# Clustered attention and token mixing: transposes of the row maxima two units later, logits two units earlier, a weight chunk converted in six stages instead of four

## The chip, the cores and the metric

The kernel runs on one core of one Trainium2 chip. The metric is the device time in microseconds (us) of one execution; of several, the median is given. Five engines run their own instruction queues in order and wait for one another through semaphores: PE (TensorE, matrix products), DVE (VectorE), ACT (ScalarE), POOL (GpSimd), and SP (SyncE), which here issues nearly all DMAs.

## The reference

```python
def _attn_ref(q, k, v, centroids):          # q, k, v: 4 x 8 heads x 768 x 64, float32
    q_n = q / (norm(q) + 1e-06); k_n = ...; c_n = ...      # 16 centroids for each head
    q_assign = argmax(einsum('bhsd,hcd->bhsc', q_n, c_n), -1)
    k_assign = argmax(einsum('bhsd,hcd->bhsc', k_n, c_n), -1)
    mask = q_assign[:, :, :, None] == k_assign[:, :, None, :]
    scores = where(mask, scale * q @ k.T, -1e9)
    attn = exp(scores - max(scores, -1))
    return (attn / (sum(attn, -1) + 1e-09)) @ v

def _moe_ref(x, w_theta, w_tok_r, w_tok_i, w_ch):   # x: the heads side by side, 4 x 768 x 512
    theta = x @ w_theta
    y = einsum('ts,bsd->btd', w_tok_r, x * cos(theta)) + einsum('ts,bsd->btd', w_tok_i, x * sin(theta))
    u = x + y
    return u + maximum(u @ w_ch, 0.0)
```

A query sees only the keys that fall to the same centroid. The four weight matrices arrive as float64.

## The kernel before

**Pairs and units.** The 32 heads are worked off as 16 pairs of heads, one head on partitions 0 to 63 and the other on 64 to 127. A pair has 12 *units*: two halves of 384 queries, each against six tiles of 128 keys. For a unit PE makes the scores of 128 keys by 384 queries for both heads (`sc`, four products: high and low parts of q and k, and a product of `mk` and `mq` that carries the mask and the row maximum), ACT takes the exponential into `at`, POOL adds up `at` tiles into `acc` for the softmax sums, and PE multiplies `at` with v (`av`). All of PE's work on one pair lasts some 30 us.

**The maxima, 12 units ahead.** The row maximum is subtracted inside the scores product, so it is made one pair ahead (`LEAD = 12`): PE makes `m` (128 queries by 768 keys), DVE reduces it (`nm`, L364). After three turns of the loop the six columns of a half are complete; `shift_row` (L368) transposes them on PE (`mt`, L372), ACT copies them (`mr`, L374) and two small DMAs write them as a row into `mq` (L376). The first scores product of that half reads the row.

**The loop.** One turn of the loop at L561 takes two units. PE's order in a turn is: the scores of the first unit for both heads; the second unit's scores of head 0 beside an `m` of head 1; eight `av` products; the extra work that is due at the even unit; the second unit's scores of head 1 beside an `m` of head 0; the extra work due at the odd unit. In what follows a turn is named by its even unit within the pair: turn 0, 2, 4, 6, 8, 10. The functions `at_unit` and `stages` put the extra work into a table by unit; a generator's stages are run up to the next `yield`, one for each number of a tuple. `in_order` (L507) then pins the program order on every engine, so that order, and nothing else, is what each queue runs.

**The extra work of a pair**, by unit within the pair (P is the pair whose scores run): 

- assignment to centroids (`assign`, `A_UNITS`), for P+3: load of q and k (`raw`) at 4, logits `lg` (L248) and their copy `lgs` at 8, transposes `lt` (L259) with `mxl` and `eq` (L262, L264) at 10, `eq` times weights and `rr` (L268, L270) at 11; for P+2: `rt` (L292) and `ri` at 2, DMA `rd` at 3, four DMAs `clq`/`clk` at 4, `mq` (L305) at 7, `mk` (L307) at 9;
- high and low parts of q and k of P+2: ACT copies at 0 and 2 (L324), POOL subtractions `lq` at 2 and `lk` at 4 (L328);
- `shift_row` at 6 (first half of P+1) and at 0 (second half of P); the load of v at 7;
- softmax sums of P-1: `sm` on PE and `se` on ACT at 4, small DMAs at 6, 8, 9 and 10; the scaling of the result of P-2 on POOL (L472) at 1 and its DMA at 3;
- one weight chunk (`early_weights`, 14 chunks, `to_f32` and `split_w`): DMA of the float64 words at 0; at 4 the magnitude on ACT (`Abs`, L132), a clamp (L133) and a shift (L135) on DVE; at 6 two bit operations on DVE (L138, L140); at 8 the rounded high part on ACT (L149) and the low part on POOL (L150). Eight chunks have 512 columns (`w_theta`, `w_ch`), six have 768.

**Buffers that matter here.** The tiles `m`, `lg`, `lt`, `rt`, `mt` and `sm` take turns in one pool of two PSUM buffers (`m_tile`, through `bank`): a tile can be written once the tile before the last has been read. The scores have three PSUM banks. `raw` has three buffers, so the load of a pair's k waits for the POOL subtraction `lq` of the pair before. A chunk's float64 words and its result have one buffer each.

After the 16 pairs the mixing stage follows (L596 on): for each 128-token tile theta, sine and cosine, two mixing products (`y`) and the channel product (`cp`, `cy`).

Of the kernel before, what the change touches and what calls it, by code (L numbers as in the profile page):

```python
# [21 lines left out]
LEAD = 12  # L22
# [18 lines left out]
def kernel(  # L41
# [23 lines left out]
    NT = S // P  # L65
# [49 lines left out]
    def to_f32(src, cols, new):  # L115

        raw, w = new()
        w = w[:, 0:cols]
        if src.dtype == F32:
            nc.sync.dma_start(out=w, in_=src)
            return w
        raw = raw.bitcast(I32)[:, 0:2 * cols]
        nc.sync.dma_start(out=raw, in_=src.bitcast(I32))
        raw = raw.rearrange("p (n t) -> p n t", t=2)
        low, high = raw[:, :, 0], raw[:, :, 1]
        wi = w.bitcast(I32)  # L130
        yield
        nc.scalar.activation(out=w, in_=high.bitcast(F32), func=AF.Abs)  # L132
        nc.vector.tensor_scalar(  # L133
            out=w, in0=w, scalar1=F64_LEAST, scalar2=F64_MOST, op0=ALU.max, op1=ALU.min)
        nc.vector.tensor_scalar(  # L135
            out=wi, in0=wi, scalar1=5, scalar2=2, op0=ALU.logical_shift_left, op1=ALU.logical_shift_right)
        yield
        nc.vector.scalar_tensor_tensor(  # L138
            out=wi, in0=low, scalar=29, in1=wi, op0=ALU.logical_shift_right, op1=ALU.bitwise_or)
        nc.vector.scalar_tensor_tensor(  # L140
            out=wi, in0=high, scalar=-(1 << 30), in1=wi, op0=ALU.bitwise_and, op1=ALU.bitwise_or)
        return w

    def split_w(hi, lo, src, cols, new, eng, most):

        def chunk(sl):
            w = yield from to_f32(src[:, sl], sl.stop - sl.start, new)
            yield
            nc.scalar.copy(out=hi[:, sl], in_=w)  # L149
            eng.tensor_tensor(out=lo[:, sl], in0=w, in1=hi[:, sl].bitcast(F32), op=ALU.subtract)  # L150

        n = cols // -(-cols // most)
        return [chunk(slice(c0, c0 + n)) for c0 in range(0, cols, n)]
# [21 lines left out]
    for x in range(3):  # L175
        x = (NPAIR + x) % 3
# [242 lines left out]
    def sums(pi):  # L419

        s = st[pi]
        sm = bank(f"sm{pi}")[:, 0:HS]
        for x in range(NT // TERMS):
            for j in range(2):
                for a in range(2):
                    g = 2 * j + a
                    nc.tensor.matmul(  # L427
                        sm[32 * g:32 * g + 32], lhsT=ecol, rhs=s["acc", a, x][:, j],
                        start=(x == 0), stop=(x == NT // TERMS - 1))
        se = p2.tile([P, HS], F32, tag="se", name=f"se{pi}", bufs=1)  # L430

        if pi < NPAIR - 1:
            nc.scalar.activation(out=se, in_=sm, func=AF.Identity, bias=eps)
        else:
            last_sum[0] = nc.vector.tensor_scalar_add(se, sm, 1e-9)
        yield

        sd = [dram.tile([4, HS], F32, tag=f"sd{x}", name=f"sd{x}{pi}", bufs=2) for x in range(2)]
        over = [x.rearrange("g (r n) -> (g r) n", r=32) for x in sd]
        nc.sync.dma_start(out=sd[0], in_=se.rearrange("(g r) n -> g r n", r=32)[:, 0])  # L440
        yield
        sq = p2.tile([P, 4 * HS // P], F32, tag="sq", name=f"sq{pi}")
        nc.sync.dma_start(out=sq, in_=over[0])
        yield
        nc.vector.reciprocal(out=sq, in_=sq)
        nc.sync.dma_start(out=over[1], in_=sq)
        yield
        s["rb"] = p1.tile([P, 2, HS], F32, tag="rb", name=f"rb{pi}")
        for j in range(2):
            last_load[0] = nc.sync.dma_start(  # L450
                out=s["rb"][64 * j:64 * j + 64],
                in_=sd[1][2 * j:2 * j + 2].unsqueeze(0).broadcast_to([64, 2, HS]))
# [15 lines left out]
    def normalise(pi):  # L468
        b, p = divmod(pi, NP)
        s = st.pop(pi)  # L470

        (nc.gpsimd if pi < NPAIR - 2 else nc.vector).tensor_tensor(  # L472
            out=s["xt"], in0=s["xt"], in1=s["rb"], op=ALU.mult)
        yield
        nc.sync.dma_start(out=xT_d[b][:, p], in_=s["xt"].rearrange("p a s -> p (a s)"))

    def early_weights():
        for c in range(NCT):
            yield from split_w(*w_th[c], w_theta[c * P:(c + 1) * P], DM, raw_pair, nc.gpsimd, CKE)
        for t in range(EARLY):  # L480
            for w, src in ((w_r, wrT), (w_i, wiT)):
                yield from split_w(*w[t], src[t * P:(t + 1) * P], S, raw_pair, nc.gpsimd, CKE)
        for c in range(NCT):
            yield from split_w(*w_c[c], w_ch[c * P:(c + 1) * P], DM, raw_pair, nc.gpsimd, CKE)
# [8 lines left out]
    def at_unit(u, fn, *a):  # L493
        todo.setdefault(u, []).append((fn, a))

    def stages(units, gen):

        for u in units:
            at_unit(u, lambda: next(gen, None))
        at_unit(units[-1] + 1, run, gen)  # L500
# [15 lines left out]
                tail[ins.engine] = ins.name  # L516


    A_UNITS = (-8, -4, -2, -1, 2, 3, 4, 7, 9)
    HI_UNITS = dict(q=0, k=2)  # L520
    LO_UNITS = dict(q=2, k=4)
    W_UNITS = (4, 6, 8)
    W_EVERY = 12
    def prepare(pi, gen):
        u = NU * (pi - 2)
        stages([u + k + (4 if pi == 1 and k < 0 else 0) for k in A_UNITS[1 if pi == 1 else 0:]], gen)
        for n in "qk":
            at_unit(u + HI_UNITS[n], part_hi, pi, n)
            at_unit(u + LO_UNITS[n], part_lo, pi, n, nc.gpsimd)
# [14 lines left out]
    for pi in range(NPAIR):  # L544
        u = NU * pi
        if pi > 0:
            prepare(pi, g1 if pi == 1 else assign(pi))
            at_unit(u - NU + 7, load_v, pi)
        for a in range(2):
            at_unit(u + a * NT - LEAD + NT, shift_row, pi, a)  # L550
        stages([u + NU + k for k in SUMS], sums(pi))
        stages([u + NU + k for k in NORM], normalise(pi))
    for x, gen in enumerate(early_weights()):
        u = W_EVERY * x
        stages([u] + [u + k for k in W_UNITS], gen)


    idle = ps_av.tile([P, 512], F32, tag="av", name="idle")
# [1 line left out]
    u = -LEAD  # L560
# [175 lines left out]
    def add_y(b, c0, c1):  # L736

        xT, n = xts[b], c1 - c0
        uh, ul = (u_tile(f"u{x}{b}_{c0}")[:, :, 0:n] for x in "hl")
        for d in range(NCT):  # L740
            x = xT[:, d, c0:c1]
            for n0, n1, _ in cuts(b, d, c0, c1):
                nc.vector.tensor_tensor(
                    out=xT[:, d, n0:n1], in0=y_at(b, d, n0, n1), in1=xT[:, d, n0:n1], op=ALU.add)
            nc.scalar.copy(out=uh[:, d, :], in_=x)  # L745
            nc.gpsimd.tensor_tensor(out=ul[:, d, :], in0=x, in1=uh[:, d, :].bitcast(F32), op=ALU.subtract)  # L746
        return uh, ul
# [54 lines left out]
    u = None  # L802
    for part in range(S // PW):
# [4 lines left out]
        u = add_y(B - 1, part * PW, (part + 1) * PW)  # L808
# [28 lines left out]
def _build(arrays):  # L837
    import concourse.bacc as _bacc
    import concourse.tile as _tile
    from concourse import mybir as _mybir  # L840

    nc = _bacc.Bacc("TRN2", target_bir_lowering=False, num_devices=1)
    args = []
    for name in _NAMES:
        a = arrays[name]
        args.append(nc.dram_tensor(f"in_{name}_dram", a.shape, _mybir.dt.from_np(a.dtype), kind="ExternalInput").ap())
    B, H, D, S = arrays["qT"].shape
    args.append(nc.dram_tensor("out_0_dram", (B, H * D, S), _mybir.dt.float32, kind="ExternalOutput").ap())
    with _tile.TileContext(nc, schedule_with_timeline_sim=True) as tc:
        kernel(tc, *args)  # L850
    return nc
# [10 lines left out]
```

## Time and profile before

| | |
|---|---|
| median of 3 runs | 877.84 us (877.35 to 878.13) |
| the profiled execution | 880.9 us, its span 879.1 us |
| mean granted TensorE clock | 0.979 |
| lead-in of the maxima | from about 14 to 37 us of the span |
| units of the 16 pairs | from about 37 to 497 us |
| mixing stage at a steady pace | from about 572 us to the end |

The page gives busy time by engine, then the span in 40 slices of 22 us, then the chain of work that ended last. In the views by instruction each row has the start in the span, the duration, the engine, the line, output and inputs, and in brackets the idle time of the engine before it with what ended it. `PEld` is the weight load of a matrix product.

### The profile page before, as it was taken

How to read it: one execution, taken by the hardware profiler on the slowest of the kernel's cores; microseconds unless marked ns; L12 is line 12 of the kernel's file. 1: busy time of each engine (PE TensorE's matmuls, PEld its weight loads, DVE VectorE, ACT ScalarE, POOL GpSimd, SP SyncE). 2: the span in 40 equal slices, each digit the busy share in tenths (PEclk: the TensorE clock that was granted, in tenths of full speed). 3: DMA queues.
4: the chain of work that ended last, by engine and by line, in shares of the span. 5: the costliest groups of instructions: out<-in, count | busy, mean ns of one | idle time of the engine just before them, and what ended most of it. 6: DMA issues, size and time to landing. Idle time of an engine off the chain costs nothing.

```text
span 879.1 us, 14379 instructions
## 1 busy us (share of the span) xinstructions
PE 813.5 (93%) x5688; PEld 594.2 (68%) x5688; DVE 501.3 (57%) x660; ACT 383.2 (44%) x787; POOL 462.7 (53%) x298
## 2 busy tenths in 40 slices
PE   4899989898898899889899989999999999999998
PEld 2465555555555555555555547789888988899998
DVE  5686676678668667766864158944333442253322
ACT  3255554555554455455544456453233323323220
POOL 3186767677785786767576646454122412241231
PEclk9699999999999999999999998999999999999999
DMA  2122322322331332232223135200300030001001
GB/s 92 55 80 89 107 61 85 117 93 82 118 113 50 113 118 63 98 99 85 74 68 118 47 122 167 73 1 1 144 1 1 11 133 1 1 27 46 1 7 67
DMA packets 29648, 62.21 MB, mean 71 GB/s; under 512 B 8932, under 2 KB 14156, under 8 KB 29196
## 3 DMA queue, kind: packets, MB, share of 16 engines
q1 hardware_dynamic: 29436, 60.89, 21.3%
q8 instruction: 45, 0.74, 0.3%
q10 hardware_dynamic: 144, 0.39, 0.1%
q14 instruction: 23, 0.19, 0.1%
HBM read 48.20 MB, written 12.96 MB: 70 GB/s over the span
## 4 chain that ended last, share of the span: by engine, by line
PE 71%; DVE 19%; issue 4%; ACT 3%; DMA 2%; POOL 0%; SPq 0%; DVEq 0%; POOLq 0%; ACTq 0%
PE y L732 20%; PE sc L342 12%; PE av L460 11%; PE m L342 7%; PE tp L665 6%; DVE nm L364 6%; PE cy L755 4%; DVE w L133 3%; PE sm L427 3%; DVE eq L268 2%; PE cp L755 2%; PE lg L248 2%; ACT w L132 1%; DVE eq L264 1%; DVE mxl L262 1%
## 5 line engine op out<-in xcount | busy, mean ns | idle before, releaser
L364 DVE TENSOR_REDUCE nm<-m 128x1 f32<-128x768 f32 x192 | 181.2, 952 | 93.6 <-PE m L342 82.6
L395 ACT ACTIVATE at<-sc 128x384 f32<-128x384 f32 x384 | 172.1, 491 | 111.3 <-PE sc L342 78.1
L406 POOL TENSOR_TENSOR acc<-at,at 128x768 f32<-128x768 f32 x64 | 120.3, 1880 | 122.4 <-ACT at L395 122.4
L342 PE MATMUL m<-hk,hq 64*128 64x384 f32 x384 | 150.0, 404 | 12.0 <-DVE nm L364 11.9
L460 PE MATMUL av<-at,vt 128*64 128x384 f32 x768 | 146.3, 501 | 0.0
L406 POOL TENSOR_TENSOR acc<-acc,at 128x768 f32<-128x768 f32 x64 | 122.3, 1910 | 25.0 <-ACT at L395 23.8
L342 PE MATMUL m<-mk,mq 64*128 64x384 f32 x384 | 129.7, 351 | 0.4 <-ACT mk L286 0.4
L342 PE MATMUL sc<-hq,hk 64*128 64x384 f32 x384 | 120.7, 385 | 5.8 <-ACT at L395 4.0
L686 POOL TENSOR_TENSOR zlc<-ab,zhc 128x512 fp32r<-128x512 f32 x24 | 32.2, 1340 | 175.6 <-ACT zhc L684 163.6
L342 PE MATMUL sc<-lq,hk 64*128 64x384 f32 x384 | 106.7, 348 | 0.0
L342 PE MATMUL sc<-mq,mk 64*128 64x384 f32 x384 | 103.0, 339 | 0.0
L342 PE MATMUL sc<-hq,lk 64*128 64x384 f32 x384 | 102.7, 338 | 0.0
L342 PEld LDWEIGHTS sc<-hq,hk 64*128 64x128 f32 x384 | 60.2, 187 | 53.6 <-issue 26.5
L342 PEld LDWEIGHTS m<-hk,hq 64*128 64x128 f32 x384 | 72.8, 196 | 24.1 <-DVE nm L364 22.8
L460 PEld LDWEIGHTS av<-at,vt 128*64 128x64 f32 x768 | 46.9, 137 | 59.5 <-issue 58.3
L342 PEld LDWEIGHTS m<-mk,mq 64*128 64x128 f32 x384 | 73.5, 198 | 0.8 <-ACT mk L286 0.8
L669 DVE TENSOR_SCALAR kk<-tp 128x512 int32<-128x512 f32 x24 | 16.5, 689 | 99.7 <-PE tp L665 99.7
L342 PEld LDWEIGHTS sc<-hq,lk 64*128 64x128 f32 x384 | 60.4, 188 | 0.0
L342 PEld LDWEIGHTS sc<-mq,mk 64*128 64x128 f32 x384 | 60.4, 188 | 0.0
L342 PEld LDWEIGHTS sc<-lq,hk 64*128 64x128 f32 x384 | 60.3, 189 | 0.0
L746 POOL TENSOR_TENSOR ul<-xT,uh 128x384 fp32r<-128x384 f32 (+1 forms) x36 | 33.8, 964 | 42.5 <-ACT uh L745 35.8
L660 ACT COPY xn<-xp 128x512 f32<-128x512 f32 x24 | 14.1, 585 | 89.8 <-PE xp L658 89.8
(152 smaller groups left out, 1666.9 us busy)
## 6 DMA issues: line engine op xcount, KB each, us to landing
rawq<-in_qT_dram SPq DMA_DIRECT2D x16, 384.0 KB
vt<-in_v_dram SPq DMA_DIRECT2D x16, 384.0 KB
rb<-sd SPq DMA_DIRECT2D x32, 192.0 KB
xT_d<-xt SPq DMA_DIRECT2D x16, 384.0 KB
rawk<-in_kT_dram SPq DMA_DIRECT2D x15, 384.0 KB
xT<-xT_d SPq DMA_DIRECT2D x3, 1536.0 KB
out_dram<-ot SPq DMA_DIRECT2D x24, 192.0 KB
w<-in_wrT_dram SPq DMA_DIRECT2D x3, 768.0 KB
```

The costliest lines, as they stand in the source:

```text
L133: nc.vector.tensor_scalar(out=w, in0=w, scalar1=F64_LEAST, scalar2=F64_MOST, op0=ALU.max, op1=ALU.min)
L342: nc.tensor.matmul(out, lhsT=stat[r, cols], rhs=mov[r, over], start=start, stop=stop)
L364: nc.vector.tensor_reduce(out=s["nm", a][:, j, i // 2:i // 2 + 1], in_=s["m", j][:, :, 0:HS], op=ALU.max, axis=AX.XY, negate=True)
L395: last_exp[0] = nc.scalar.activation(out=s["at", a, i][:, j], in_=s["sc", j], func=AF.Exp, scale=SCALE)
L406: last_acc[0] = nc.gpsimd.tensor_tensor(out=s["acc", a, x], in0=prev, in1=at, op=ALU.add)
L427: nc.tensor.matmul(sm[32 * g:32 * g + 32], lhsT=ecol, rhs=s["acc", a, x][:, j], start=(x == 0), stop=(x == NT // TERMS - 1))
L460: nc.tensor.matmul(s["av"][64 * j:64 * j + 64], lhsT=s["vt"][:, i, j, :], rhs=s["at", a, i][:, j], start=(i == 0), stop=(i == NT - 1))
L665: nc.tensor.matmul(tp, lhsT=xx[:, c, :], rhs=w_th[c][k], start=(n == 0), stop=(n == 3 * NCT - 1))
L686: nc.gpsimd.tensor_tensor(out=zl, in0=tr, in1=zh.bitcast(F32), op=ALU.subtract)
L732: nc.tensor.matmul(y_at(b, d, c0, c1), lhsT=zz[:, d * P:(d + 1) * P], rhs=ww[:, c0:c1], start=first and lead, stop=last, skip_group_check= ...
L746: nc.gpsimd.tensor_tensor(out=ul[:, d, :], in0=x, in1=uh[:, d, :].bitcast(F32), op=ALU.subtract)
L755: nc.tensor.matmul(cp, lhsT=w_c[d][k][:, e * P:(e + 1) * P], rhs=uu[:, d, :], start=(n == 0), stop=(n == 3 * NCT - 1), skip_group_check=True)
```

## The change

Three tables and two `yield`s are changed. `shift_row` is due two units later (8 and 2 of the pair instead of 6 and 0; the very first one stays). The loads of q and k and the logits are due two units earlier (2 and 6 instead of 4 and 8). The weight chunk has six stages: DMA at 8 of the pair before, magnitude at 10 of the pair before, clamp and shift at 0, first bit operation at 2, second at 4, high and low part at 6.

```diff
@@ to_f32
         yield
         nc.scalar.activation(out=w, in_=high.bitcast(F32), func=AF.Abs)
+        yield
         nc.vector.tensor_scalar(
             out=w, in0=w, scalar1=F64_LEAST, scalar2=F64_MOST, op0=ALU.max, op1=ALU.min)
         nc.vector.tensor_scalar(
@@
         nc.vector.scalar_tensor_tensor(
             out=wi, in0=low, scalar=29, in1=wi, op0=ALU.logical_shift_right, op1=ALU.bitwise_or)
+        yield
         nc.vector.scalar_tensor_tensor(
             out=wi, in0=high, scalar=-(1 << 30), in1=wi, op0=ALU.bitwise_and, op1=ALU.bitwise_or)
         return w
@@
-    A_UNITS = (-8, -4, -2, -1, 2, 3, 4, 7, 9)
+    A_UNITS = (-10, -6, -2, -1, 2, 3, 4, 7, 9)
-    W_UNITS = (4, 6, 8)
+    W_UNITS = (8, 10, 12, 14, 16, 18)
     W_EVERY = 12
     def prepare(pi, gen):
         u = NU * (pi - 2)
-        stages([u + k + (4 if pi == 1 and k < 0 else 0) for k in A_UNITS[1 if pi == 1 else 0:]], gen)
+        stages([u + k + (6 if pi == 1 and k < 0 else 0) for k in A_UNITS[1 if pi == 1 else 0:]], gen)
@@
-            at_unit(u + a * NT - LEAD + NT, shift_row, pi, a)
+            at_unit(u + a * NT - LEAD + NT + (2 if u + a else 0), shift_row, pi, a)
@@
     for x, gen in enumerate(early_weights()):
-        u = W_EVERY * x
-        stages([u] + [u + k for k in W_UNITS], gen)
+        stages([W_EVERY * (x - 1) + k for k in W_UNITS], gen)
```

From L134 on the changed kernel's line numbers are one or two higher: the clamp is its L134, the shift L136, the bit operations L139 and L142, `nm` L366, `mt` L374.

What this does to the order of three queues is shown at the places that the prediction speaks of. In the names, `_0` and `_1` stand for the head and the last number tells one buffer's use from the next.

VectorE over the turns 0 to 6 of a pair, before: five maxima, then clamp and shift of the chunk at unit 4, both bit operations at unit 6.

```order
L364 TENSOR_REDUCE nm_1809<-m_1_1810 128x1
L364 TENSOR_REDUCE nm_1809<-m_0_1837 128x1
L364 TENSOR_REDUCE nm_1809<-m_1_1867 128x1
L364 TENSOR_REDUCE nm_1809<-m_0_1890 128x1
L364 TENSOR_REDUCE nm_1809<-m_1_1921 128x1
L133 TENSOR_SCALAR w_1834<-w_1834 128x768
L135 TENSOR_SCALAR w_1834<-w_1834 128x768
L364 TENSOR_REDUCE nm_1809<-m_0_1960 128x1
L364 TENSOR_REDUCE nm_1987<-m_1_1988 128x1
L138 SCALAR_TENSOR_TENSOR w_1834<-w_1833,w_1834 128x768
L140 SCALAR_TENSOR_TENSOR w_1834<-w_1833,w_1834 128x768
```

VectorE over the same turns, now:

```order
L366 TENSOR_REDUCE nm_1813<-m_1_1814 128x1
L134 TENSOR_SCALAR w_1721<-w_1721 128x768
L136 TENSOR_SCALAR w_1721<-w_1721 128x768
L366 TENSOR_REDUCE nm_1813<-m_0_1834 128x1
L366 TENSOR_REDUCE nm_1813<-m_1_1864 128x1
L139 SCALAR_TENSOR_TENSOR w_1721<-w_1720,w_1721 128x768
L366 TENSOR_REDUCE nm_1813<-m_0_1898 128x1
L366 TENSOR_REDUCE nm_1813<-m_1_1929 128x1
L142 SCALAR_TENSOR_TENSOR w_1721<-w_1720,w_1721 128x768
L366 TENSOR_REDUCE nm_1813<-m_0_1962 128x1
L366 TENSOR_REDUCE nm_1989<-m_1_1990 128x1
```

Clamp and shift stand four maxima earlier, between the two maxima of turn 0; the bit operations stand apart from each other, one in turn 2 and one in turn 4. The half's last maximum (`m_0_1960` before, `m_0_1962` now) no longer has clamp and shift ahead of it.

TensorE after the eight `av` products of turn 0, before: a transpose of maxima, whose tile lies between those of `m_1_1810` and `m_0_1837` in the rotation of two buffers.

```order
L460 MATMUL av_1704<-at_1735,vt_1318 64x384 x2
L460 MATMUL av_1704<-at_1750,vt_1318 64x384 x2
L372 MATMUL mt_1826<-identf,nm_1631 6x128
L342 MATMUL sc_1_1836<-hq_140,hk_142 128x384
L342 MATMUL m_0_1837<-hk_151,hq_149 128x384
```

TensorE after the `av` products of turn 2, now:

```order
L462 MATMUL av_1875<-at_1798,vt_1677 64x384 x2
L462 MATMUL av_1875<-at_1811,vt_1677 64x384 x2
L374 MATMUL mt_1880<-identf,nm_1633 6x128
L294 MATMUL rt_1886<-identf,rr_1796 24x128
L344 MATMUL sc_1_1897<-hq_140,hk_142 128x384
L344 MATMUL m_0_1898<-hk_151,hq_149 128x384
```

The transpose has left turn 0, where nothing stands between `av` and the next scores any more, and stands in turn 2 ahead of `rt`. Turn 0 has two tiles of the rotation now, turn 2 has four.

The DMA queue of SP over one pair, before:

```order
L376 DMA mq_144<-mr_1828 1x3x128 x2
L127 DMA w_1833<-in_wrT_dram 128x1536
L475 DMA xT_d_60<-xt_1291 128x768
L297 DMA rd_1902<-ri_1885 24x128
L302 DMA clq<-rd_1902 16x768 x2
L302 DMA clk<-rd_1902 16x768 x2
L242 DMA rawq_1952<-in_qT_dram 128x768
L242 DMA rawk_1954<-in_kT_dram 128x768
L440 DMA sd_2005<-se_1945 4x384
L376 DMA mq_153<-mr_2010 1x3x128 x2
```

The same queue now, from the DMA of the second half's maxima on:

```order
L378 DMA mq_144<-mr_1882 1x3x128 x2
L244 DMA rawq_1892<-in_qT_dram 128x768
L244 DMA rawk_1894<-in_kT_dram 128x768
L477 DMA xT_d_60<-xt_1293 128x768
L299 DMA rd_1910<-ri_1888 24x128
L304 DMA clq<-rd_1910 16x768 x2
L304 DMA clk<-rd_1910 16x768 x2
L442 DMA sd_2007<-se_1953 4x384
L319 DMA vt_2033<-in_v_dram 128x768
L445 DMA sq_2068<-sd_2007 128x12
L378 DMA mq_153<-mr_2072 1x3x128 x2
L127 DMA w_2076<-in_wiT_dram 128x1536
```

The two loads `raw` stand ahead of `xT_d`, `rd`, `clq` and `clk` now, and the chunk's load stands behind the first half's maxima, in turn 8.

## The prediction

> **What bounds the kernel now.** First the chain of waits that ended last, by line, from the page; then the busy time of the stages; then what PE waited for while the units ran.
>
> ```profile
> PE y L732 20%; PE sc L342 12%; PE av L460 11%; PE m L342 7%; PE tp L665 6%; DVE nm L364 6%; PE cy L755 4%; DVE w L133 3%; PE sm L427 3%; DVE eq L268 2%; PE cp L755 2%; PE lg L248 2%; ACT w L132 1%; DVE eq L264 1%; DVE mxl L262 1%
> 37.40:497.00 459.60, 420.00 (x3336) 254.92 (x3334) 316.28 (x335) 237.70 (x527) 325.18 (x178) 0.99 0.28 89
> 572.00:879.00 307.00, 303.99 (x1876) 277.75 (x1875) 111.52 (x199) 97.41 (x172) 88.06 (x78) 1.00 0.09 32
> PE mt L372 <- DVE nm L364: 24.4, 13, 2.0
> PE m L342 <- DVE nm L364: 10.6, 26, 0.6
> PE sc L342 <- ACT at L395: 2.6, 8, 0.5
> ```
>
> The chain is PE's nearly throughout, but it passes through the clamp `w` L133 and the magnitude L132, which are no part of attention. In a row of stretches the columns are: stretch, length, then busy us of PE, PE's weight loads, DVE, ACT and POOL, clock, DMA share, GB/s. The mixing stage (572 to 879) has PE busy 303.99 of 307.00 and is not touched. In the units PE stands idle 459.6 - 420.0 = 39.6 us, and three waits make up nearly all of that: 24.4 in 13 waits of the transpose `mt` for the maxima, 10.6 of `m` for the maxima, 2.6 of the scores for exponentials (each row: sum, times, longest). So about 40 us is the most that better order can win in idle time.
>
> Where in a pair it sits, by six turns (4, 6, 8, 10, 0, 2), cut at the starts of `av`:
>
> ```profile
> 195.52:201.24 5.72, 5.44 (x50) 2.90 (x48) 2.19 (x2) 3.17 (x7) 5.72 (x4) 1.00 0.50 145
> 201.24:207.89 6.65, 4.44 (x35) 2.75 (x33) 6.58 (x7) 2.25 (x6) 3.05 (x3) 1.00 0.16 57
> 207.89:212.81 4.92, 4.92 (x42) 2.81 (x40) 3.87 (x6) 2.95 (x7) 4.50 (x3) 1.00 0.30 81
> 212.81:217.25 4.44, 4.44 (x37) 2.88 (x35) 4.23 (x6) 1.61 (x5) 3.53 (x3) 1.00 0.29 90
> 217.25:222.22 4.97, 4.37 (x34) 2.75 (x33) 3.56 (x4) 3.18 (x9) 1.84 (x2) 1.00 0.08 16
> 222.22:226.31 4.09, 4.09 (x35) 2.56 (x33) 1.92 (x2) 2.79 (x7) 4.09 (x3) 1.00 0.61 229
> ```
>
> The stretch from 201.24 holds the `mt` of turn 6: PE is idle 6.65 - 4.44 = 2.21 us while DVE works 6.58 of 6.65. The one from 217.25 holds the second `mt` and is idle 0.60. The timeline says why:
>
> ```profile
> 198.53 0.58 ACT L433 ACTIVATE se<-sm,eps 128x384 f32<-128x384 f32 x1 [2.35 <-PE sm L427]
> 199.01 0.89 ACT L132 ACTIVATE w<-w 128x768 f32<-128x768 f32 x1
> 199.47 1.84 POOL L328 TENSOR_TENSOR lk<-rawk,hk 128x768 fp32r<-128x768 f32 x1
> 200.00 1.73 DVE L133 TENSOR_SCALAR w<-w 128x768 f32<-128x768 f32 x1 [3.38 <-ACT w L132]
> 201.27 2.14 POOL L406 TENSOR_TENSOR acc<-acc,at 128x768 f32<-128x768 f32 x1
> 201.77 2.05 DVE L135 TENSOR_SCALAR w<-w 128x768 int32<-128x768 int32 x1
> 203.74 1.81 DVE L364 TENSOR_REDUCE nm<-m 128x1 f32<-128x768 f32 x2
> 204.74 0.27 PE L372 MATMUL mt<-identf,nm 128*6 128x128 f32 x1 [1.99 <-DVE nm L364]
> L133 DVE TENSOR_SCALAR w<-w x14: 426/1733/1839, 48.1 to 447.7; 128x512 f32<-128x512 f32 x8, 128x768 f32<-128x768 f32 x6
> L268 DVE TENSOR_TENSOR eq<-eq,wc x16: 358/1648/1671, 10.5 to 433.9; 128x384 bf16<-128x384 bf16 x16
> ```
>
> DVE stands 3.38 us with the clamp at the head of its queue, because the magnitude is queued on ACT behind `se`, and `se` behind `sm`. Then clamp and shift take 1.73 and 2.05 us, the half's last maximum comes after them, and `mt` after that. The durations are waits too: the clamp ends 0.42 us after POOL's `lk` ends (201.31), the shift 0.41 us after `acc` ends (203.41). The last two rows (ns: least, median, most) agree: a clamp took 426 at least and 1733 in the median, `eq` 358 and 1648. So some DVE instructions run only between POOL instructions.
>
> **The change part by part.** The sum is made against the profiled execution, 880.9 us with a span of 879.1; the median of the runs is 877.84, 3.1 below, and the difference is carried over to it.
>
> *Transposes back, chunk stages apart.* In turn 6 DVE has no chunk work left, and `mt`, a turn later, finds its maxima done: all 24.4 us go. Of the 10.6 us, 13 waits of 0.60 (7.8) are those of turn 0, where `m` took the buffer of the tile before `mt` and so waited for the maximum made just before. Without `mt` it takes the buffer of a tile read a turn earlier, and they go; the 0.2 that turn 6 has goes with the bit operations. In turn 8 `mt` now stands where `lg` stood, and `mq` L305 still delays one maximum, so I keep some: 9 us won. With the magnitude gone from behind `se`, 2 of the 2.6 us go. Turn 6, with `lg` in place of `mt`, should last what turn 8 lasted, 4.92, and turn 8 what turn 2 lasted, 4.09: together 9.0 for 11.57, or 2.56 less where the idle time was 2.2. The 0.4 beyond it is PE's restart; between 0 and 13 x 0.4 = 5, I take 3.
>
> *Half clock.* After some of these stalls the granted clock is halved:
>
> ```profile
> 138.80:142.20 3.40, 1.42 (x9) 0.40 (x8) 3.37 (x4) 1.03 (x3) 2.14 (x2) 1.00 0.34 136
> 142.20:145.60 3.40, 3.40 (x18) 2.90 (x20) 2.96 (x5) 0.75 (x2) 0.65 (x1) 0.50 0.14 18
> 452.80:456.20 3.40, 3.21 (x19) 2.97 (x20) 2.96 (x5) 0.62 (x2) 1.03 (x1) 0.51 0.23 52
> ```
>
> There are four such stretches in the units, the first and the last shown; each follows a turn 6 in which PE was busy some 1.4 to 2.0 of 3.4 us. One costs at most 1.7 us, the four 0 to 6.8; without the stalls I take 6.
>
> [...]
>
> *Lead-in.* `rt` of pair 1 waited 3.57 us there for `rr` in the turn of `lt`; now it comes a turn later:
>
> ```profile
> 23.65 0.39 PE L292 MATMUL rt<-identf,rr 128*24 128x128 f32 x1 [3.57 <-DVE rr L270]
> ```
>
> DVE still has to do the same work, so 0 to 3; I take 1.5.
>
> *What it adds.* Won so far: 24.4 + 9 + 2 + 6 + 3 + 1.5 = 45.9. Against it:
>
> ```profile
> 216.38 1.83 POOL L406 TENSOR_TENSOR acc<-acc,at 128x768 f32<-128x768 f32 x1 [0.91 <-ACT at L395]
> 218.93 0.95 DVE L364 TENSOR_REDUCE nm<-m 128x1 f32<-128x768 f32 x1
> 219.94 0.44 PE L342 MATMUL m<-hk,hq 64*128 64x384 f32 x1 [0.60 <-DVE nm L364]
> 221.34 1.83 POOL L406 TENSOR_TENSOR acc<-at,at 128x768 f32<-128x768 f32 x1 [3.13 <-ACT at L395]
> 209.40 0.78 PE lg L248 x8
> 205.33 1.42 SPq L376 DMA_DIRECT2D mq<-mr  x2
> 220.96 0.41 SPq L127 DMA_DIRECT2D w<-in_wrT_dram  x1
> 222.00:225.20 3.20, 3.20 (x27) 1.90 (x25) 1.25 (x2) 2.16 (x6) 3.20 (x3) 1.00 0.72 249
> 215.74 0.49 ACT L395 ACTIVATE at<-sc 128x384 f32<-128x384 f32 x1 [2.27 <-PE m L342]
> 195.91 1.83 POOL L328 TENSOR_TENSOR lq<-rawq,hq 128x768 fp32r<-128x768 f32 x1
> 199.05 0.38 SPq L242 DMA_DIRECT2D rawk<-in_kT_dram  x1
> L138 DVE SCALAR_TENSOR_TENSOR w<-w,w x14: 675/678/945, 53.1 to 453.1; 128x512 int32<-128x512 int32 x8, 128x768 int32<-128x768 int32 x6
> ```
>
> Turn 2 now has `mt` and `rt`, two small copies on ACT ahead of the copy of k, and an `m` that needs the buffer of `mt`: between 0 and 0.6 us in a pair, I take 0.3, 13 x 0.3 = 4.
>
> Magnitude in turn 10: queued behind it on ACT is the turn's last exponential, for which PE's next scores wait. `mt` starts where `lg` did, at 209.4. In turn 6 the two `mq` DMAs were out 205.33 + 1.42 - 204.74 = 2.0 us after `mt`, so the chunk's load is issued at 211.4. Before, 4.2 us lay between issue (220.96) and the end of its traffic (225.20, 249 GB/s): 215.6, and with 0.89 for the magnitude 216.5. The exponential was ready at 215.74 and would be at 215.2, as `mt` is 0.5 shorter than `lg`. So it is late by 1.3 us for the six wide chunks; the narrow ones move two thirds of it, land 1 us earlier, have two thirds of the magnitude, and cost nothing. 6 x 1.3 = 7.8; the bounds are 0 and, if DMAs collide for 1 us in every pair, 22.
>
> Clamp and shift in turn 0: POOL is free from 218.21 (216.38 + 1.83) to 221.34, and DVE gets to the clamp at 219.88. Free of POOL the two need some 0.9 us narrow (twice 0.43), in time for the maximum of head 0. But with the wait of `m` (0.60) and `mt` (0.27) gone the next `acc` comes 0.9 us earlier, at some 220.4, and if it starts ahead of the shift, the shift waits for it. Between 0 and 2.0 in a pair; I take 3 in all and make the loss of this race a rival. The bit operations have DVE idle around them in turns 2 and 4 (1.92 busy of 4.09, 2.19 of 5.72): nothing.
>
> Loads of k: `lq` has to end first (197.74), and the load left at 199.05 before, so it gains only 1.3 us, while `lg` wants it where `mt` began to wait, 204.74 - 1.99 = 202.75, instead of at 209.4. Half a chunk's 3.2 us of traffic, 1.6, with 0.38 issue and 1 us start is 3 of the 5 us; 2 are left. `xT_d`, `rd`, `clq` and `clk` stand behind it on SP. I take 2 in all.
>
> Costs: 4 + 7.8 + 3 + 2 = 16.8. Net 45.9 - 16.8 = 29.1 less: 851.8 for the profiled execution, **848.7 for the median**.
>
> **The rivals.** *The block moves with its instructions.* If the shift of turn 0 falls behind `acc`, it ends about 1.83 + 0.43 us later, two maxima are late, and `mt` and `rt` in turn 2 both need the buffers that these read: about 2.0 us in a pair. For it: POOL is at work 4.09 of 4.09 us in turn 2 and the margin is tenths. Against it: the free stretch begins 1.7 us before DVE arrives, and where the wide chunk's magnitude delays the exponentials, `acc` comes later. In 8 to 13 pairs, less the 3 counted, 13 to 23 more: about 867.
>
> [...]
>
> *Slower: the loads of k come too late.* [...] With 2 us of slack, lateness beyond it is PE's wait at `lg` in 13 pairs. From 2.0 + 29.1 / 13 = 4.2 us on the change loses; at 5 us the time is about 888. [...]
>
> *The wait only changes its name.* If DVE were short of time, another reader of its maxima would wait instead: within 0.2% of before. But DVE is busy 22.3 of 30.8 us in the six rows above.
>
> **How the numbers follow.** Forecast 0.62 (832 to 858), the block moves 0.20 (858 to 874), slower 0.07, wait renamed 0.04, faster than 832 because the added costs fail to show 0.07. Leaving out the ends gives 832 to 868 for 8 in 10. A measurement of this kernel tells 0.2%, 1.8 us, from no change. Faster 0.88, same 0.05, slower 0.07.
>
> **What would show it.** Right: no `mt` among PE's waits; clamp and shift near 0.4 to 0.6 us in turn 0; the stretch of turn 6 near 4.9; no half clock between 40 and 490 us; a period of a pair near 28.5 us with narrow chunks and 29 with wide ones. Wrong: a median shift of 1.7 us or more with PE waiting in turn 2 (first rival), `lg` waiting for a DMA (second), or ACT's magnitude waiting for its load longer than 2 us in every pair.

## The result, and the profile after

The changed kernel takes **848.34 us** in the median (844.85 to 849.76); the kernel before took 877.99 beside it. The ratio is 0.9642, with a 95% interval of 0.9592 to 0.9692. The forecast was 848.7. Its sum came out right, but as the experiments show, not because each of its terms did.

The profiled execution took 848.33 us with a span of 846.4. The stage of the units, and what PE waited for in it (the views that showed 459.60 and 420.00 us, and 24.4, 10.6 and 2.6 us, before):

```profile
36.00:466.00 430.00, 412.67 (x3336) 249.97 (x3338) 293.77 (x332) 239.51 (x527) 337.94 (x178) 0.99 0.32 94
...
PE sc L344 <- ACT at L397: 14.1, 18, 2.3
PE m L344 <- DVE nm L366: 1.6, 1, 1.6
```

The stage is 29.6 us shorter. PE's idle time in it fell from 39.6 to 17.3 us, and PE's busy time by 7.3. No transpose waits any more, and 9.0 of the 10.6 us of `m` are gone; but the scores' wait for exponentials grew from 2.6 to 14.1 us. One pair by turns (4, 6, 8, 10, 0, 2), here with a narrow chunk (columns as before: stretch, length, busy us of PE, PE's weight loads, DVE, ACT, POOL, clock, DMA share, GB/s):

```profile
360.58:365.89 5.31, 5.31 (x50) 2.90 (x48) 3.74 (x3) 2.45 (x6) 5.31 (x4) 1.00 0.60 152
365.89:370.61 4.72, 4.72 (x43) 2.66 (x41) 2.40 (x3) 3.26 (x8) 4.16 (x4) 1.00 0.36 127
370.61:374.69 4.08, 4.08 (x35) 2.56 (x33) 2.70 (x5) 2.06 (x6) 3.92 (x3) 1.00 0.34 99
374.69:379.79 5.10, 4.58 (x37) 2.88 (x35) 4.00 (x7) 2.47 (x6) 2.69 (x2) 1.00 0.41 136
379.79:383.90 4.11, 4.00 (x35) 2.47 (x33) 2.68 (x4) 2.97 (x6) 1.82 (x2) 1.00 0.20 60
383.90:388.25 4.35, 4.35 (x37) 2.77 (x35) 4.02 (x3) 2.66 (x7) 4.35 (x3) 1.00 0.00 1
```

Turn 6 takes 4.72 us (6.65 before), turn 0 takes 4.11 (4.97). Turn 10 went the other way, 5.10 for 4.44, with PE idle 0.52. The timeline of that turn, with the `mt` of turn 8 ahead of it and the clamp and the shift in turn 0 behind it:

```profile
372.05 0.27 PE L374 MATMUL mt<-identf,nm 128*6 128x128 f32 x1
...
374.16 0.36 SPq L127 DMA_DIRECT2D w<-in_w_ch_dram  x1
...
377.26 0.34 PE L344 MATMUL sc<-mq,mk 64*128 64x384 f32 x1
377.72 0.67 ACT L132 ACTIVATE w<-w 128x512 f32<-128x512 f32 x1 [2.38 <-DMA w<-in_w_ch_dram]
378.28 1.25 ACT L397 ACTIVATE at<-sc 128x384 f32<-128x384 f32 x3
378.65 0.35 DVE L270 TENSOR_TENSOR eq<-eq,wc 128x384 bf16<-128x384 bf16 x1
378.82 0.44 PE L344 MATMUL sc<-hq,hk 64*128 64x384 f32 x1 [0.52 <-ACT at L397]
378.91 1.83 POOL L408 TENSOR_TENSOR acc<-acc,at 128x768 f32<-128x768 f32 x1 [2.14 <-ACT at L397]
...
380.77 0.42 DVE L134 TENSOR_SCALAR w<-w 128x512 f32<-128x512 f32 x1
381.23 0.43 DVE L136 TENSOR_SCALAR w<-w 128x512 int32<-128x512 int32 x1
```

ACT stands 2.38 us at the magnitude, whose load was issued only 3.56 us before; the exponentials (their scores are complete at 377.60) queue behind it, and PE behind them. Clamp and shift run at 0.42 and 0.43 us, free of POOL. Over the whole execution the shift never met POOL (median and most at the second and third number):

```profile
L136 DVE TENSOR_SCALAR w<-w x14: 426/428/560, 39.1 to 408.9; 128x512 int32<-128x512 int32 x8, 128x768 int32<-128x768 int32 x6
```

An earlier pair, with a wide chunk, shows two more waits that were not there before, both for DMAs that stand behind the loads of q and k in SP's queue:

```profile
189.35 0.34 SPq L244 DMA_DIRECT2D rawk<-in_kT_dram  x1
189.74 0.42 SPq L477 DMA_DIRECT2D xT_d<-xt  x1
190.21 0.40 SPq L299 DMA_DIRECT2D rd<-ri  x1
...
194.24 0.78 SPq L304 DMA_DIRECT2D clq<-rd  x2
194.25 0.48 ACT L468 COPY xt<-av 128x384 f32<-128x384 f32 x1 [1.63 <-DMA xT_d<-xt]
...
197.80 2.13 DVE L307 TENSOR_SCALAR mq<-clq,mcl 128x768 fp32r<-128x768 f32 x1 [1.63 <-DMA clq<-rd]
199.86 0.94 DVE L366 TENSOR_REDUCE nm<-m 128x1 f32<-128x768 f32 x1
200.85 0.44 PE L344 MATMUL m<-hk,hq 64*128 64x384 f32 x1 [1.59 <-DVE nm L366]
```

### The profile page after: what moved, and what is told of

Its sections match the earlier page's. It is cut to its first block, busy times and chain, and to the rows that moved or that the text cites. A ratio compares the mean times of both kernels' runs of the same rounds, so it can differ in the third digit from the quotient of the medians.

```text
span 846.4 us, 14454 instructions
## 1 busy us (share of the span) xinstructions
PE 802.8 (95%) x5688; PEld 586.7 (69%) x5688; DVE 480.2 (57%) x660; ACT 385.2 (46%) x787; POOL 474.7 (56%) x298
## 4 chain that ended last, share of the span: by engine, by line
PE 66%; DMA 10%; DVE 6%; ACT 5%; POOL 5%; issue 5%; SPq 1%; ACTq 0%; POOLq 0%; DVEq 0%
PE y L734 21%; PE sc L344 13%; PE av L462 10%; PE tp L667 6%; PE cy L757 4%; PE m L344 3%; DMA xT_d<-xt 3%; POOL acc L408 3%; PE cp L757 2%; ACT at L397 2%; PE sm L429 2%; DMA w<-in_w_ch_dram 2%; DMA w<-in_wiT_dram 2%; DMA w<-in_wrT_dram 2%; DVE nm L366 1%
## 5 line engine op out<-in xcount | busy, mean ns | idle before, releaser
L366 DVE TENSOR_REDUCE nm<-m 128x1 f32<-128x768 f32 x192 | 182.7, 954 | 118.9 <-PE m L344 98.2
L408 POOL TENSOR_TENSOR acc<-at,at 128x768 f32<-128x768 f32 x64 | 129.1, 2017 | 64.5 <-ACT at L397 62.3
L344 PE MATMUL m<-hk,hq 64*128 64x384 f32 x384 | 147.7, 394 | 4.6 <-DVE nm L366 4.6
L408 POOL TENSOR_TENSOR acc<-acc,at 128x768 f32<-128x768 f32 x64 | 125.0, 1954 | 39.9 <-ACT at L397 38.5
L344 PE MATMUL sc<-hq,hk 64*128 64x384 f32 x384 | 118.9, 387 | 17.3 <-ACT at L397 15.5
L344 PEld LDWEIGHTS sc<-hq,hk 64*128 64x128 f32 x384 | 57.3, 186 | 77.3 <-issue 36.1
L344 PE MATMUL sc<-lq,hk 64*128 64x384 f32 x384 | 102.4, 343 | 0.0
L344 PE MATMUL sc<-mq,mk 64*128 64x384 f32 x384 | 100.2, 337 | 0.0
L344 PE MATMUL sc<-hq,lk 64*128 64x384 f32 x384 | 100.1, 337 | 0.0
L344 PEld LDWEIGHTS sc<-mq,mk 64*128 64x128 f32 x384 | 57.7, 187 | 0.0
L344 PEld LDWEIGHTS sc<-lq,hk 64*128 64x128 f32 x384 | 57.5, 188 | 0.0
L344 PEld LDWEIGHTS sc<-hq,lk 64*128 64x128 f32 x384 | 57.5, 187 | 0.0
```

Source lines behind the costliest of these rows:

```text
L344: nc.tensor.matmul(out, lhsT=stat[r, cols], rhs=mov[r, over], start=start, stop=stop)
L366: nc.vector.tensor_reduce(out=s["nm", a][:, j, i // 2:i // 2 + 1], in_=s["m", j][:, :, 0:HS], op=ALU.max, axis=AX.XY, negate=True)
L408: last_acc[0] = nc.gpsimd.tensor_tensor(out=s["acc", a, x], in0=prev, in1=at, op=ALU.add)
```

## The experiments

All times are medians; each ratio is to the kernel before on the same chip, with its 95% interval. By ratio, 0.01 is 8.8 us.

### The three parts apart

**Transposes alone** (`e1_transposes_only`):

```diff
--- the kernel before
-            at_unit(u + a * NT - LEAD + NT, shift_row, pi, a)
+            at_unit(u + a * NT - LEAD + NT + (2 if u + a else 0), shift_row, pi, a)
```

> The kernel before with the transposes of the maxima two units later and nothing else. Theory: in turn 6 the maximum behind clamp and shift is late as before (203.74 in the trace of before); with mt gone from turn 6, the m of head 0 takes the buffer that this very maximum frees, so PE waits there instead of at mt. Only the 13 waits of 0.6 us in turn 0 and some tenths go: 866 to 874 us, with PE's wait renamed from mt to m, 20 us or more in sum. Rival: the wait is worth what it says, 24.4 + 7.8 us and the half clock go with mt alone: 842 to 850 us.

Measured: 905.39 us, ratio 1.0318 (1.0292 to 1.0343), 28 us slower than before. Neither expectation holds. The wait is renamed, as the first one said, but it also grows. What PE waited for in the units:

```profile
PE lg L248 <- DVE nm L364: 22.7, 13, 1.8
PE m L342 <- DVE nm L364: 15.3, 12, 1.4
PE mt L372 <- DVE nm L364: 13.1, 12, 1.3
```

and in one pair, on PE:

```profile
415.01 0.44 PE L342 MATMUL m<-hk,hq 64*128 64x384 f32 x1 [1.35 <-DVE nm L364]
...
419.71 0.27 PE L372 MATMUL mt<-identf,nm 128*6 128x128 f32 x1 [0.91 <-DVE nm L364]
421.79 0.51 PE L248 MATMUL lg<-rawq,cb 128*32 128x384 f32 x1 [1.80 <-DVE nm L364]
```

With DVE's block still in turn 4, `m` of turn 6 waits for the late maximum in place of `mt`. In turn 8 `mt` and `lg` together need the buffers of two maxima, and these are late as well, since bit operations and `mq` stand ahead of them on DVE. Three stalls in a pair instead of two; and they bring half clock, here 6.8 us of it after a stretch in which PE was busy 1.51 of 3.40 us:

```profile
116.50:119.90 3.40, 1.51 (x9) 0.37 (x5) 3.40 (x4) 0.70 (x3) 2.81 (x2) 1.00 0.00 0
119.90:126.70 6.80, 5.98 (x34) 4.19 (x36) 2.65 (x5) 2.60 (x6) 1.85 (x2) 0.50 0.03 4
```

The mean clock of that execution is 0.972, against 0.979 before. From 40 us to the end of the units there are nine stretches of half clock, 37.5 us, against four with 13.7 before. Half of the difference is some 12 us, an estimate; together with the three waits above, which are 16 us longer than the 24.4 and 10.6 of before, it makes up the 28.

**Chunk alone** (`e2_chunk_only`):

```diff
--- the changed kernel
-    A_UNITS = (-10, -6, -2, -1, 2, 3, 4, 7, 9)
+    A_UNITS = (-8, -4, -2, -1, 2, 3, 4, 7, 9)
...
-            at_unit(u + a * NT - LEAD + NT + (2 if u + a else 0), shift_row, pi, a)
+            at_unit(u + a * NT - LEAD + NT, shift_row, pi, a)
```

> The kernel before with the weight chunk in six stages and nothing else. Theory: DVE's block of 3.38 + 3.8 us in turn 4 is the cause, so mt in turn 6 finds its maxima done: 24.4 us of mt, 2.8 of m, 2 of the scores and most of the half clock (6) go, the 7.8 us of m in turn 0 stay, and ACT's magnitude waiting for its load costs 8 to 12: 850 to 858 us. Rival: the transposes have to move too, 866 us or more.

Measured: 836.76 us, ratio 0.9536 (0.9514 to 0.9559). The chunk part by itself is better than the whole change, by more than I had expected of it. PE's waits in the units:

```profile
PE m L344 <- DVE nm L366: 7.7, 13, 0.6
PE sc L344 <- ACT at L397: 1.9, 4, 0.5
```

The 13 waits of turn 0 are left, 7.7 us as expected; every wait of `mt` is gone although the transposes have not moved.

**Logits alone** (`e3_logits_only`): the kernel before with the loads and the logits of the next pair two units ahead.

```diff
--- the kernel before
-    A_UNITS = (-8, -4, -2, -1, 2, 3, 4, 7, 9)
+    A_UNITS = (-10, -6, -2, -1, 2, 3, 4, 7, 9)
...
-        stages([u + k + (4 if pi == 1 and k < 0 else 0) for k in A_UNITS[1 if pi == 1 else 0:]], gen)
+        stages([u + k + (6 if pi == 1 and k < 0 else 0) for k in A_UNITS[1 if pi == 1 else 0:]], gen)
```

> The kernel before with the loads of q and k and the logits two units earlier and nothing else. Theory: it takes no wait away, since mt in turn 6 still waits for the late maximum; the loads now stand ahead of xT_d and clq/clk on SP, which costs 0 to 4 us: 876 to 882 us. Rival: by leaving turn 8 the logits take load off PE there, 870 us or less.

Measured: 884.1 us, ratio 1.0053 (1.0022 to 1.0084): some 0.5% slower, just above the 876 to 882 that the theory gave. The rival is out. PE's waits show why it takes nothing away:

```profile
PE mt L372 <- DVE nm L364: 22.6, 12, 2.0
PE m L342 <- DVE nm L364: 7.7, 13, 0.6
PE lg L248 <- DVE nm L364: 7.6, 13, 0.6
```

**The change without its logits part** (`e4_no_logits`): loads and logits where they were before the change.

```diff
--- the changed kernel
-    A_UNITS = (-10, -6, -2, -1, 2, 3, 4, 7, 9)
+    A_UNITS = (-8, -4, -2, -1, 2, 3, 4, 7, 9)
...
-        stages([u + k + (6 if pi == 1 and k < 0 else 0) for k in A_UNITS[1 if pi == 1 else 0:]], gen)
+        stages([u + k + (4 if pi == 1 and k < 0 else 0) for k in A_UNITS[1 if pi == 1 else 0:]], gen)
```

> The changed kernel without its logits part (loads at 4 and logits at 8 as before, so mt and lg both stand in turn 8). Theory: the logits part brings nothing and costs the waits that xT_d, now behind the loads, lays on ACT's copy xt (12.9 us of ACT's idle time in the changed kernel's trace) and on clq (4.6 us); without it these go: 839 to 847 us. Rival: mt and lg in one turn make four tiles in two buffers and PE waits there, 850 us or more.

Measured: 835.68 us, ratio 0.9526 (0.9505 to 0.9547), below the 839 to 847 of the theory; the rival is out. On top of the other two parts the logits part costs 0.0116, some 10 us. And beside the chunk part alone (0.9536) the transposes bring nothing that can be told from zero, while the chunk's load stands at unit 8: PE's 7.7 us of `m` are gone, but its wait for exponentials is 5.3 us in place of 1.9.

### What the clamp's place is worth

`e5_clamp_later`: clamp and shift one unit later.

```diff
--- the changed kernel
-    W_UNITS = (8, 10, 12, 14, 16, 18)
+    W_UNITS = (8, 10, 13, 14, 16, 18)
```

> The changed kernel with clamp and shift one unit later (unit 1 instead of 0 of the pair), behind the second maximum of turn 0, where POOL runs acc and the scaling back to back. It prices the first rival of the prediction. Theory: clamp and shift now take about 1.8 to 2.3 us each instead of 0.4 to 0.6, the next maximum comes some 3 us later, rt in turn 2 waits for its buffer, 2.0 to 2.6 us in each of 13 pairs: 872 to 882 us. Rival: DVE has slack there, as it is idle 40% of the time: within 3 us of the changed kernel, 845 to 851 us.

Measured: 895.95 us, ratio 1.0194 (1.0154 to 1.0235), worse than the theory's 872 to 882. Clamp, and what PE waited for first:

```profile
L134 DVE TENSOR_SCALAR w<-w x14: 1981/2014/2140, 40.2 to 453.9; 128x512 f32<-128x512 f32 x8, 128x768 f32<-128x768 f32 x6
...
PE rt L294 <- DVE nm L366: 35.1, 14, 2.7
```

One unit later the same instruction takes 2014 ns instead of 419 (medians), and `rt` waits 35.1 / 14 = 2.5 us in a pair, the mechanism of the forecast's first rival. The price of it in time was higher than the wait itself, 48 us. The mean clock fell to 0.979: there are nine stretches of half clock from 40 us to the end of the units, 34.1 us, where the changed kernel has two with 6.8. Half of the difference is some 14 us, an estimate, and with the 35.1 of `rt` it covers the price.

### Two late loads, each hidden by the other

`e6_load_early`: the chunk's load at unit 6 in place of 8.

```diff
--- the changed kernel
-    W_UNITS = (8, 10, 12, 14, 16, 18)
+    W_UNITS = (6, 10, 12, 14, 16, 18)
```

> The changed kernel with the chunk's load two units earlier (6 instead of 8 of the pair before). It prices the wait of the magnitude for its load. Theory: ACT's 35 to 39 us of waiting for the load go, and with them most of PE's 14.1 us of scores waiting for exponentials: 836 to 842 us. Rival: the wait is hidden by DVE's work on eq and rr in the same turn, or the load collides with the small DMAs of turn 6: 846 us or more.

Measured: 852.15 us, ratio 0.969 (0.9654 to 0.9726), not better than the changed kernel. The magnitude no longer waits; ACT's `xt` and DVE's `mq` do, more than in the changed kernel (12.9 and 4.6 us there). DVE also waits for the small DMA `sq`, which stands behind all of these in SP's queue. PE waits behind them:

```profile
ACT xt L468 <- DMA xT_d<-xt: 20.6, 10, 3.4
...
DVE sq L447 <- DMA sq<-sd: 10.4, 11, 1.8
...
DVE mq L307 <- DMA clq<-rd: 9.4, 7, 2.3
...
PE m L344 <- DVE nm L366: 12.3, 10, 1.6
```

`e7_raw_behind`: the loads of q and k at unit 3, behind `xT_d` and `rd`.

```diff
--- the changed kernel
-    A_UNITS = (-10, -6, -2, -1, 2, 3, 4, 7, 9)
+    A_UNITS = (-9, -6, -2, -1, 2, 3, 4, 7, 9)
```

> The changed kernel with the loads of q and k one unit later (3 instead of 2), so that they stand behind xT_d and rd on SP. Theory: ACT's copy xt no longer waits for xT_d (12.9 us of idle time in the changed kernel), mq no longer for clq (4.6), and PE gains 2 to 5 us: 843 to 846 us. Rival: lg in turn 6 then waits for its load, 850 us or more; or the waits were hidden, 847 to 849 us.

Measured: 847.64 us, ratio 0.9633 (0.9593 to 0.9673). No wait for `xT_d` or `clq` is left in its trace, and nothing is won: PE still waits 13.8 us for exponentials behind the magnitude.

`e8_both`: both edits together.

```diff
--- the changed kernel
-    A_UNITS = (-10, -6, -2, -1, 2, 3, 4, 7, 9)
+    A_UNITS = (-9, -6, -2, -1, 2, 3, 4, 7, 9)
...
-    W_UNITS = (8, 10, 12, 14, 16, 18)
+    W_UNITS = (6, 10, 12, 14, 16, 18)
```

> The changed kernel with both: the chunk's load at 6 and the loads of q and k at 3. Theory: the gains add, 833 to 840 us. Rival: one wait covered the other, and it is no better than the better of the two by itself.

Measured: 831.46 us, ratio 0.9456 (0.9424 to 0.9488). Alone, one edit brought nothing and the other nothing or a loss; together they bring 0.0186, some 16 us. PE waits 2.3 us for exponentials and 0.3 for a load:

```profile
PE sc L344 <- ACT at L397: 2.3, 5, 0.5
```

`e9_logits_back`: logits in turn 8 again, loads still at unit 2.

```diff
--- the changed kernel
-    A_UNITS = (-10, -6, -2, -1, 2, 3, 4, 7, 9)
+    A_UNITS = (-10, -4, -2, -1, 2, 3, 4, 7, 9)
...
-        stages([u + k + (6 if pi == 1 and k < 0 else 0) for k in A_UNITS[1 if pi == 1 else 0:]], gen)
+        stages([u + k + (4 if pi == 1 and k < 0 else 0) for k in A_UNITS[1 if pi == 1 else 0:]], gen)
```

> The changed kernel with the logits back in turn 8 (unit 8), while the loads of q and k stay at unit 2, ahead of xT_d and clq on SP. It splits the 12.6 us by which the logits part made the change worse. Theory: it is the place of lg: with lg in turn 8, 0.8 us more lie between the transpose, behind whose two DMAs the chunk's load is issued, and the magnitude that waits for that load; PE's wait for exponentials falls from 14 to some 6 us: 835 to 841 us. Rival: it is the loads' place in the DMA queue, which this kernel keeps: 845 to 850 us.

Measured: 852.28 us, ratio 0.9694 (0.9658 to 0.9731). My theory falls: with the loads ahead of `xT_d` and `clq` it does not help to have `lg` in turn 8. But `e7`, with the loads behind and `lg` in turn 6, is no better, so the logits part costs in both ways, and either is enough.

`e12_result_ahead`: `e6` with only `xT_d` put ahead of the loads.

```diff
--- e6
-NORM = (13, 15)
+NORM = (13, 14)
```

> The changed kernel with the chunk's load at 6 and, of the DMAs that stand behind the loads of q and k, only the result xT_d put ahead of them (unit 2 instead of 3); rd, clq and clk stay behind. It tells which of the two waits behind the loads is the one that costs: ACT's copy xt waiting for xT_d (20.6 us of ACT idle in the kernel with the early chunk load alone, 852 us) or mq on DVE waiting for clq (9.4 us). If xT_d: 830 to 838 us. If clq: 845 us or more.

Measured: 836.9 us, ratio 0.954 (0.9494 to 0.9587). Against `e6` that is 0.015, and `e8`, which moves `rd` too, has another 0.0084, by intervals that lie just apart (0.9494 and 0.9488). So with the chunk's load at 6, most of what the loads cost goes away with the place of `xT_d`. The wait for `sq` shrank with it, from 10.4 us in 11 waits to 3.8 in 5, so the two were not told apart.

### A version that beats both

`e10_no_logits_load_early`: transposes and chunk part of the change, no logits part, the chunk's load at unit 6.

```diff
--- e4
-    W_UNITS = (8, 10, 12, 14, 16, 18)
+    W_UNITS = (6, 10, 12, 14, 16, 18)
```

> The changed kernel without its logits part (loads at 4, logits at 8) and with the chunk's load at unit 6: both known costs off the path at once. Theory: what PE waits for exponentials (5.3 us without the logits part) falls to 2 or 3, nothing takes its place: 829 to 833 us, like the kernel with the loads behind xT_d. Rival: the load in turn 6 meets the loads of q and k, which are issued in turn 4 here, and holds up the small DMAs: 836 us or more.

Measured: **829.84 us**, ratio 0.9449 (0.9418 to 0.948). The units:

```profile
36.00:450.00 414.00, 409.17 (x3369) 247.39 (x3367) 293.34 (x336) 242.47 (x528) 343.19 (x179) 1.00 0.30 99
```

PE is idle 4.8 of 414 us; there is little left to win by order.

`e11_chunk_only_load_early`: the same with the transposes where they were.

```diff
--- e2
-    W_UNITS = (8, 10, 12, 14, 16, 18)
+    W_UNITS = (6, 10, 12, 14, 16, 18)
```

> Only the chunk part of the change, transposes and logits as before, and the chunk's load at unit 6. It tells what the transposes bring where no load is late. Theory: the 13 waits of 0.6 us of m in turn 0 stay, so it is 5 to 9 us slower than the kernel that also moves the transposes: 836 to 840 us. Rival: DVE's and ACT's work makes up for it and the transposes bring nothing: 829 to 833 us.

Measured: 846.1 us, ratio 0.9618 (0.9588 to 0.9649), some 15 us slower than `e10` and slower than the chunk part with its load at 8 (0.9536). Both expectations are off. DVE says where it comes from:

```profile
DVE sq L447 <- DMA sq<-sd: 9.3, 12, 1.9
```

The transposes in turn 6 put their `mq` DMAs, which wait for ACT, ahead of the chunk's load; the load then goes out just ahead of the small `sq` DMA, and DVE stands at the reciprocal of `sq` with the maxima behind it: `m` waits 15.0 us in 19 waits. In `e10` the load leaves earlier and this wait does not appear. `e6` has the same wait with the transposes moved, as its loads hold up the queue. That the order on SP is what does it was read from the traces, not tried by itself.

## Why the prediction was right, and where it was wrong

- **Clamp and shift away from turn 4: right, and with the chunk's load at unit 8 it is the whole gain.** All 24.4 us of `mt` and 9.0 of `m` went, as summed. But the forecast put this down to the transposes and the chunk stages together. `e2` shows that the chunk part does it alone, all but 7.7 us of `m`, which the transposes take away without a gain in time (`e4`); `e1` shows that the transposes alone lose 28 us. "The wait only changes its name" was given 0.04 as the fate of the change; it is what happens to its first part when made alone.
- **Shapes of the turns: right with narrow chunks, not with wide ones.** In the narrow pair above, turn 6 was put at 4.92 and measured 4.72, turn 8 at 4.09 and 4.08, turn 2 at 0.3 above 4.09 and 4.35. In the wide pair with the two further waits, turn 8 took 5.96 us and the six turns 29.75:

```profile
197.18:203.14 5.96, 4.37 (x35) 2.75 (x33) 4.28 (x5) 1.77 (x5) 4.34 (x3) 1.00 0.51 131
186.66:216.41 29.75, 27.35 (x224) 16.38 (x222) 21.74 (x24) 16.03 (x36) 23.40 (x13) 1.00 0.35 102
```

Over the execution a pair with a narrow chunk took 27.6 to 28.1 us (28.5 forecast), one with a wide chunk 28.7 to 31.4 (29 forecast).

- **Half clock and restart: about half of the clock's term came.** 6 us were forecast for half clock, with none left between 40 and 490 us, and 3 for what the forecast called PE's restart, an estimate of 0.4 us a stall (2.56 less 2.2). Two of the four stretches are left, at 176.1 and 237.6, behind the two longest waits for the magnitude (PE idle 2.28 and 1.66 us). The first of them, and what went before:

```profile
172.72:176.13 3.41, 1.13 (x14) 0.81 (x12) 1.87 (x4) 1.86 (x4) 0.44 (x1) 1.00 0.09 30
176.13:179.54 3.41, 3.41 (x14) 1.07 (x11) 1.98 (x3) 0.67 (x2) 1.39 (x1) 0.50 0.37 109
```

Two stretches fewer are worth 3.4 of the 7.3 us by which PE's busy time fell, at the forecast's 1.7 for one, an estimate; the rest was not taken apart, so no run shows the restart by itself. The stretches before half clock here and in `e1` have PE at work, 1.13 of 3.41 and 1.51 of 3.40 us, as the forecast's row had before the change, 1.42 of 3.40.

- **Lead-in: 1.5 forecast.** The first scores product starts at 34.2 us of the span where it started at 36.6; in `e2` it starts at 36.9, so this part does not come with the chunk stages.
- **The race in turn 0: right that it is won.** No shift lost it (median 428 ns, most 560), so the 3 us held back for it were not spent. `e5` prices the loss at 2.5 us a pair where I put 2.0, and more in all.
- **The magnitude behind its load: right in kind, mis-sized.** I had 7.8 us less 2 for the wait of the scores, and none of it in narrow chunks. The wait grew by 11.5. In the trace PE waits 8.6 us behind the six wide chunks, 1.4 each and close to the 1.3 of the forecast, but also 3.7 behind seven narrow ones, 0.5 each. `e7` against `e8` puts the price of it all, with the other wait out of the way, at 16 us. The step that failed is the narrow chunks' "cost nothing", by a few tenths in each of its three parts. In the narrow pair above, the load was issued 2.11 us after `mt` (2.0 forecast) and used 3.56 us after that (3.2 forecast), and the exponential was due at 377.60, 5.55 us after `mt`, where the forecast had 215.2 - 209.4 = 5.8. The forecast's own sign of being wrong, a magnitude that waits longer than 2 us in every pair, came in 13 of 14.
- **The loads of k: wrong.** 2 us were set aside for the whole logits part, with `lg` as the one that would wait. `lg` did not wait; `xT_d`, `rd` and `clq`, named as standing behind the loads but not priced, did. `e4` puts the logits part at some 10 us. What failed is that I priced a moved DMA by its own consumer only, not by those of the DMAs that it is put ahead of. It is not the only price: in `e7`, where nothing waits for `xT_d` or `clq` any more, the kernel is no faster, since with `lg` gone from turn 8 the magnitude is late all the same.
- **The bit operations: "nothing" was right in time, wrong in how.** They took 2274 and 2045 ns in the median where they took 678 and 693 before, beside POOL's instructions (below); DVE had the room.

So the sum came out right by luck, because two errors met: the chunk part is worth about 41 us (0.0464), more than the whole I forecast, and the logits part takes back about 10. There was a third: the sum was made for the profiled execution, which became 32.6 us shorter (880.9 to 848.33) where 29.1 was forecast. The 3.1 us by which the profile before lay above the median were carried over, but the changed kernel's profile lies at its median, and that makes up most of the difference.

Of the chunk part's gain, from the first scores product to the last `av`, PE is idle 11.7 us in `e2` where it was idle 41.0 before, and busy 423.9 where it was 436.9. No half clock follows a stall there (granted clock 1.00 from 37 to 457 us), which is 6.8 of those 13.0 us at 1.7 for a stretch. The other 6 us were not taken apart.

## What to carry to other kernels

In these traces an instruction that waited at the head of its engine's queue held up what stood behind it (DVE 3.38 us at the clamp before, ACT 2.38 us at the magnitude after); give such an instruction a stage of its own, where its input is already there, before moving the reader that complains. When a DMA is moved up in a queue, price the consumers of everything that it is put ahead of. Two late inputs can hide each other, so that mending one shows nothing: look at what the wait turned into before giving the edit up.

## What the runs showed of the hardware

The two bit operations of the chunk (two inputs, `w<-w,w`) stood before where POOL was idle: the first took 678 ns in the median and 945 at most, the second 693 and 959. In their new places they take some three times that (ns: least, median, most; the first two rows are from before):

```profile
L140 DVE SCALAR_TENSOR_TENSOR w<-w,w x14: 691/693/959, 53.8 to 453.8; 128x512 int32<-128x512 int32 x8, 128x768 int32<-128x768 int32 x6
216.77 1.66 DVE L268 TENSOR_TENSOR eq<-eq,wc 128x384 bf16<-128x384 bf16 x1
...
L139 DVE SCALAR_TENSOR_TENSOR w<-w,w x14: 683/2274/2544, 41.7 to 412.6; 128x512 int32<-128x512 int32 x8, 128x768 int32<-128x768 int32 x6
L142 DVE SCALAR_TENSOR_TENSOR w<-w,w x14: 1879/2045/2466, 46.0 to 416.9; 128x512 int32<-128x512 int32 x8, 128x768 int32<-128x768 int32 x6
L270 DVE TENSOR_TENSOR eq<-eq,wc x16: 347/349/948, 10.9 to 406.3; 128x384 bf16<-128x384 bf16 x16
...
183.22 1.82 POOL L474 TENSOR_TENSOR xt<-xt,rb 128x768 f32<-128x768 f32 x1
183.32 2.53 DVE L139 SCALAR_TENSOR_TENSOR w<-w,w 128x768 int32<-128x768 int32 x1
...
184.99 2.55 POOL L408 TENSOR_TENSOR acc<-acc,at 128x768 f32<-128x768 f32 x1
```

In the wide pair of the last three rows the first one started 0.10 us after POOL's scaling of `xt` and ended at 185.85, 0.81 us after the end of that scaling (185.04). POOL pays too: the `acc` that started beside it, at 184.99, took 2.55 us, where the median of an `acc` was 1.83 before. And `eq`, at 1648 ns in the median before (in the pair of the forecast it ran from 216.77 to 218.43, beside the `acc` from 216.38 to 218.21), now takes 349: in the narrow pair above it starts at 378.65, and the `acc` only at 378.91, after POOL stood 2.14 us for the late exponential. I had not expected that gain. In `e2`, where PE waits 1.9 us for exponentials and not 14.1, the chain of work that ended last goes through `eq` again, with 1.56 to 1.58 us in a pair.

In the traces before and after, every stretch at one granted clock up to the end of the span lasted 3.41 us or a multiple of it. From 43 to 841 us of these two spans there are 455 steps of 3.41 us at full clock. Nine were followed by half clock, with PE busy 1.13 to 1.97 us in them and so none of them idle; of the others five had 1.47 to 2.00 us, and 441 had 2.01 us or more.
